# Attention scores of nine head pairs in three float32r passes, splits on GpSimd, sums' transfers on SyncE, a new order within a head pair

## The chip, the cores and the metric

The kernel runs on one core of one Trainium2 chip. The metric is the device time of one execution in microseconds, the median of the runs. Tiles have up to 128 partitions; TensorE multiplies a stationary tile (its weights) with moving columns and writes PSUM, which has eight banks of 512 float32 a partition; VectorE and ScalarE read PSUM, GpSimd works on SBUF alone, and SyncE issues transfers.

## What is computed

Attention with an additive bias of relative position, followed by a gated feed-forward block. Batch 4, 8 heads, 576 positions, head width 64, model width 512, inner width 1024, all float32.

```python
scores = scale * np.matmul(q, k.transpose(0, 1, 3, 2))
...
x = (psi_rel / psi_i)[..., None]
h = np.maximum(x @ w1 + b1, 0.0)
bias = h @ w2
scores = scores + bias.transpose(2, 0, 1)[None, :, :, :]
scores = scores - np.max(scores, axis=-1, keepdims=True)
attn = np.exp(scores)
attn = attn / (np.sum(attn, axis=-1, keepdims=True) + 1e-09)
return np.matmul(attn, v).astype(np.float32)
...
h = np.maximum(x @ w_in, 0.0)
...
    conv_out += conv_w[k][None, None, :] * hp[:, k:k + S, :]
gate = 1.0 / (1.0 + np.exp(-conv_out))
return (h * gate @ w_out).astype(np.float32)
```

## The kernel before

Three stages follow each other. In the first (to about 62 us) the bias of all heads is computed and written to DRAM; in the second (to about 282 us) attention runs; in the third the feed-forward block. The weights of the third are prepared beside the second.

Attention runs over 16 head pairs, `seq[n]` = (pair of heads p, batch b), b the faster index. The 576 queries of a pair are cut into five units: t = 0 holds the first 64 queries of both heads in one tile, t = 1 to 4 hold 128 queries each, once for each head h. One unit and head passes through these steps:

- `S` (`scores`, lines 421 to 445): queries as weights, keys as moving columns. The 576 keys lie as two halves of 288, the first on partitions 0 to 63 (a = 0), the second on 64 to 127 (a = 1), so that two matmuls of 64 rows lie side by side in the array and write the two banks of one pair of PSUM banks. The operands are float32. The unit t = 0 uses 64 columns of weights for each head, so that four matmuls lie side by side.
- `R` (`reduce`, line 452, VectorE): adds the bias tile, scales, and finds the row's extreme value, from PSUM into SBUF.
- `E` (`expo`, line 466, ScalarE): the exponential, with its row sum.
- `T` and `s` (`transposes`, `side_transposes`): 64-column transposes of the unit on TensorE as float32r, into another pair of banks; `k0`, `k1`, `k0b`, `k1b` and `c` copy them to SBUF (line 149 ScalarE, line 152 VectorE).
- `P` (`pv_parts`): the product with the values, for query columns 0 to 319 (g = 0, tile `ptx`) and 320 to 575 (g = 1, tile `pty`), five parts each; `xb` copies it out.
- `ia`, `inv`, `sm`, `rt`, `st`, `sp`, `AN`: the sums of a pair are inverted, turned, copied, stored to DRAM (`store_sums`), read back spread over partitions (`spread_sums`), and multiplied in by GpSimd (`apply_norm`, line 617).

The order of all this within one pair is written out by hand in the string `CYCLE` (line 863): each entry names a step, its unit, head and pair offset, and the engine that it runs on (P TensorE, V VectorE, A ScalarE, G GpSimd). Every engine takes its instructions in that order. The pairs of PSUM banks are given out by `take` and `done` (lines 406 to 417): a step takes, of the free pairs, the one touched longest ago, where free is judged in program order; on the chip the step then waits for those that used the pair last. `side_cols` puts side columns into spare columns of the pair of the last scores.

Queries and keys are loaded on SyncE's queue (`load`, line 205) two pairs ahead, after the step `S:4,1`; values after `P:1,4`. The bias rows of the next p are loaded as soon as the last batch's reduction of a unit has freed the tile (`load_bias`, line 231): t = 0 on SyncE's queue, t = 1 to 4 on GpSimd's, except for the first p. The sums' transfers are issued by GpSimd.

The 28 weight jobs (`job_step`, `J1`, `J2`, `J3`, `W`; `per_pair` says how many lie in each pair) bring weights into a pair of float32r tiles: VectorE shifts (line 158), ScalarE and VectorE put the parts together (159, 163), and GpSimd rounds into the first tile and subtracts for the second (lines 191, 192). The feed-forward block multiplies float32 numbers as three float32r products of such tiles (high x high, high x low, low x high; `in_products`, `ffn_out`). `x_parts` splits the attention output on GpSimd the same way.

At the end of attention, `apply_norm` of the last pairs, `split_x` of the last two weight tiles and `x_rest` (lines 637 to 645) follow on GpSimd, and TensorE multiplies the remaining 64 columns of each batch (tile `xr`) from them.

Of the kernel before, what the change touches and what calls it, by code (L numbers as in the profile page):

```python
# [9 lines left out]
F32 = mybir.dt.float32  # L10
# [8 lines left out]
def attention_ffn_kernel(  # L19
# [43 lines left out]
    arena = nc.alloc_sbuf_tensor("shared", [P, SPB * SPW], F32)  # L63
# [4 lines left out]

    sps = [[shared_at(f"s{x}{i}", [P, SPW], dt, i * SPW) for i in range(SPB)] for x, dt in (("p", F32), ("r", F32R))]
# [125 lines left out]
    with tc.manual_schedule():  # L195
        att = ExitStack()
        q_p = pool(att, "q", 2)
# [7 lines left out]
        def load(n):  # L205
            p, b = seq[n]
            qks[n] = t = q_p.tile([P, KO + S], F32, name="qk")
            keys = qk[b, p, :, KO:].rearrange("d (h a s) -> d a h s", h=2, a=2)
            for a in range(2):
                rows = slice(D * a, D * a + D)  # L210
                nc.sync.dma_start(t[rows, 0:KO], qk[b, p, :, 0:KO])
                nc.sync.dma_start(halves(t[rows, KO:]), keys[:, a])

# [14 lines left out]
        def load_bias(p, t, cuts=()):  # L231
            queue = nc.gpsimd if p and t else nc.sync
# [188 lines left out]
        def scores(n, t, h):  # L421
# [179 lines left out]
        def store_sums(n):  # L601
            rt = rts.pop(n)
            rows = r_d[n, :, TL:].rearrange("h (t x) -> h t x", x=P)
            nc.gpsimd.dma_start(rows, rt[0:8])  # L604
            nc.gpsimd.dma_start(r_d[n:n + 1, :, 0:TL], rt[8:9].rearrange("o (h x) -> o h x", h=2))

        def spread_sums(n):
            rbs[n] = rb = rb_p.tile([P, S], F32, name="rb")
            for h in range(2):
                nc.gpsimd.dma_start(rb[D * h:D * h + D], r_d[n, h:h + 1, :].to_broadcast([D, S]))  # L610
# [171 lines left out]
        slots += [[0, i - 4, 0] for i in range(4)]  # L782
        hs_ff = {}
# [45 lines left out]
        per_pair = [0, 0, 3, 0, 3, 3, 3, 0, 3, 3, 3, 0, 3, 3, 1, 0]  # L829
# [20 lines left out]
        def job_step(j, k):  # L850
# [6 lines left out]
            if k == 2:  # L857
                if j in first_job and first_job[j] % B == 0:
# [5 lines left out]
            E:1,0,0:A S:2,0,0:P S:2,1,0:P S:3,0,0:P E:1,1,0:A R:2,0,0:V S:3,1,0:P T:0,0:P R:2,1,0:V J1:0,0:V  # L864
            k1:0,0:V J2:0,0:A P:1,0,-1:P R:3,0,0:V P:1,1,-1:P E:2,0,0:A k0:0,0:A P:1,2,-1:P E:2,1,0:A R:3,1,0:V
# [384 lines left out]
```

## Time and profile before

| | |
|---|---|
| median of 3 runs | 478.18 us (477.30 to 478.56) |
| the profiled execution | 478.16 us |
| its span, first to last instruction | 476.3 us |
| TensorE matmul busy | 460.4 us (97%) |
| VectorE, ScalarE, GpSimd busy | 350.1, 312.1, 143.6 us |
| granted TensorE clock | 1.00 throughout |
| TensorE's share of the chain that ended last | 86% |

The page shows one execution. Each engine's busy time is the union of its instructions' spans; an instruction's span holds its latency, so back-to-back instructions start closer together than their mean duration. The chain that ended last is followed back from the last instruction, at each step to what released it or to the instruction before it on its engine; the time of a piece in it is what it adds to the chain, and "x8" counts instruction records. A float32 matmul appears as two records, a float32r matmul as one.

### The profile page before, as it was taken

The page shows a single profiled execution, that of the slowest core. Times are in us where ns is not written, and L with a number is a line of the kernel's source. Part 1 is how long each engine was busy: PE and PEld are TensorE (multiplying, and loading weights), DVE is VectorE, ACT ScalarE, POOL GpSimd, SP SyncE. Part 2 cuts the span into 40 slices and gives each one's busy share as a digit, 9 for nine tenths or more (in the row PEclk, how much of TensorE's full clock was granted, in tenths as well). Part 3 has the DMA queues.
Part 4 walks back from the last instruction along what each step waited for, and adds up shares of the span by engine and source line. Part 5 has one row for each costly group of instructions (what it writes and reads, how often), then busy time and mean ns, then how long its engine had stood idle before and what let it go on. Part 6 is the DMA issues. An engine that isn't in the chain of part 4 may idle for free.

```text
span 476.3 us, 10546 instructions
## 1 busy us (share of the span) xinstructions
PE 460.4 (97%) x3915; PEld 334.1 (70%) x3915; DVE 350.1 (73%) x847; ACT 312.1 (66%) x740; POOL 143.6 (30%) x216
## 2 busy tenths in 40 slices
PE   5988899999999999999999999999999999999996
PEld 3333356677667766777667778988888888888886
DVE  6999967887898799987897521892599149936971
ACT  6999876888888788988888632861354126414530
POOL 1000001344656544464568528006001500060000
PEclk9999999999999999999999999999999999999999
DMA  1799957796978968798951300002000200020002
GB/s 38 224 339 317 344 169 179 194 283 142 242 176 198 294 145 211 170 268 195 222 130 51 115 27 26 0 1 82 7 1 0 89 23 0 1 89 1 0 14 98
DMA packets 32774, 60.79 MB, mean 128 GB/s; under 512 B 7196, under 2 KB 15796, under 8 KB 32724
## 3 DMA queue, kind: packets, MB, share of 16 engines
q1 hardware_dynamic: 27860, 47.90, 36.2%
q0 software_dynamic: 4480, 11.88, 8.9%
q8 instruction: 31, 0.51, 0.5%
q10 hardware_dynamic: 384, 0.35, 0.3%
q14 instruction: 19, 0.16, 0.1%
HBM read 44.12 MB, written 15.98 MB: 126 GB/s over the span
## 4 chain that ended last, share of the span: by engine, by line
PE 86%; DVE 4%; ACT 3%; DMA 3%; POOL 2%; issue 1%; SPq 0%; POOLq 0%; DVEq 0%
PE bank L105 38%; PE pair L105 36%; PE bank L108 10%; DVE y L308 2%; DMA bias_d<-st 2%; PE pair L108 2%; DVE sp L452 1%; ACT st L351 1%; ACT y L304 1%; DMA pars<-in_par_dram 1%; ACT tl L351 1%; DMA bt<-bias_d 1%; POOL x L617 1%; ACT sp L466 0%; POOL xr L645 0%
## 5 line engine op out<-in xcount | busy, mean ns | idle before, releaser
L452 DVE CUSTOM_DVE_ANT_0 sp<-pair,bt 128x576 f32<-128x576 f32 x144 | 104.5, 750 | 27.0 <-PE pair L105 24.5
L466 ACT ACTIVATE sp<-sp,nm 128x576 f32<-128x576 f32 x144 | 110.4, 771 | 11.9 <-DVE nm L452 11.5
L105 PE MATMUL pair<-qk 64*128 64x288 f32 (+1 forms) x640 | 88.8, 426 | 2.1 <-DVE nm L452 2.0
L105 PE MATMUL pair<-xs,wi 128*128 128x512 f32 x384 | 88.9, 390 | 0.0
L105 PE MATMUL bank<-wo,g 128*128 128x512 f32 x384 | 87.7, 389 | 0.0
L105 PEld LDWEIGHTS bank<-wo,g 128*128 128x128 f32 x384 | 72.0, 188 | 14.9
L105 PEld LDWEIGHTS pair<-xs,wi 128*128 128x128 f32 x384 | 71.7, 188 | 15.3 <-issue 0.4
L108 PE MATMUL bank<-identr,sr 64*128 64x64 f32 x1184 | 65.9, 253 | 2.2 <-ACT sp L466 2.0
L108 PEld LDWEIGHTS bank<-identr,sr 64*128 64x128 f32 x1184 | 56.3, 136 | 14.1 <-issue 4.6
L1043 DVE SCALAR_TENSOR_TENSOR cv<-h,cw,cv 128x575 f32<-128x575 f32 x64 | 52.3, 818 | 12.6 <-ACT cv L1038 10.6
L105 PEld LDWEIGHTS pair<-qk 64*128 64x128 f32 (+1 forms) x640 | 47.3, 175 | 17.6 <-DVE nm L452 6.8
L666 ACT ACTIVATE h<-pair 128x512 f32<-128x512 f32 x32 | 19.1, 598 | 58.0 <-PE pair L105 58.0
L308 DVE TENSOR_SCALAR y<-tl,inv,nb 128x576 f32<-128x576 f32 (+33 forms) x112 | 47.5, 498 | 0.0
L105 PE MATMUL bank<-ptx,vt 128*64 128x320 f32 x320 | 47.0, 438 | 0.0
L105 PE MATMUL pair<-y,pars 128*32 128x512 f32 (+8 forms) x352 | 42.5, 504 | 1.7 <-DVE y L308 1.0
L191 POOL TENSOR_SCALAR xs<-x 128x512 fp32r<-128x512 f32 (+1 forms) x16 | 11.2, 700 | 103.7 <-DVE gt L1063 103.6
L105 PE MATMUL bank<-pty,vt 128*64 128x256 f32 x320 | 38.1, 384 | 0.0
L604 POOL DMA_DIRECT2D r_d<-rt x16 | 9.7, 606 | 90.1 <-DVE rt L152 90.1
L105 PEld LDWEIGHTS bank<-ptx,vt 128*64 128x64 f32 x320 | 21.4, 136 | 22.0 <-ACT ptx L149 3.1
L1049 ACT ACTIVATE cv<-cv 128x576 f32<-128x576 f32 x32 | 21.9, 684 | 21.9 <-DVE cv L1043 21.8
L1050 DVE SCALAR_TENSOR_TENSOR cv<-cv,h 128x576 f32<-128x576 f32 x32 | 24.1, 752 | 14.1 <-ACT cv L1049 14.1
L105 PEld LDWEIGHTS pair<-y,pars 128*32 128x32 f32 x352 | 15.8, 114 | 25.7 <-DVE y L308 10.2
(84 smaller groups left out, 600.1 us busy)
## 6 DMA issues: line engine op xcount, KB each, us to landing
qk<-in_qk_dram SPq DMA_DIRECT2D x32, 320.0 KB, 5.0
bias_d<-st SPq DMA_DIRECT2D x13, 607.0 KB, 5.9
bt<-bias_d POOLq DMA_DIRECT2D x24, 288.0 KB, 6.0
qk<-in_qk_dram SPq DMA_DIRECT2D x32, 144.0 KB, 5.1
rb<-r_d POOLq DMA_DIRECT2D x32, 144.0 KB, 5.1
vt<-in_v_dram SPq DMA_DIRECT2D x16, 256.0 KB, 4.0
raw_w<-in_moe_w_in_dram SPq DMA_DIRECT2D x16, 256.0 KB, 5.0
out_dram<-o SPq DMA_DIRECT2D x16, 256.0 KB, 2.0
```

Of the source, the lines that this page charges most:

```text
L105: return use(nc.tensor.matmul(o, *args, **kw), o)
L108: return use(nc.tensor.transpose(o, *args), o)
L191: first = nc.gpsimd.tensor_scalar(dst[:, 0], x, 1.0, 0.0, op0=ALU.mult, op1=ALU.add)
L308: nc.vector.tensor_scalar(y, dist[:, 0:n], inv[:, ig:ig + 1], nb1, op0=ALU.mult, op1=ALU.max)
L351: use(nc.scalar.activation(o[:, :, oo], i[:, :, ii], AF.Identity, bias=kv[:, k:k + 1], scale=inv_scale), ps)
L452: use(nc.vector.tensor_tensor_reduce(out=halves(spt[n, t][0][:, h]), in0=ps[:, :, 0:HS], in1=halves(bt[:, h]), op0=ALU.add, op1=ALU.min, s ...
L466: exps[n, t, h] = nc.scalar.activation(sp[:, h], sp[:, h], AF.Exp, bias=nm[:, h:h + 1], scale=-1.0, accum_out=sms[n][:, col:col + 1],)
L604: nc.gpsimd.dma_start(rows, rt[0:8])
L666: use(nc.scalar.activation(h[:, 0:NM], ps[:, 0], AF.Relu), ps)
L1043: nc.vector.scalar_tensor_tensor(out=cv[:, o:o + S - 1], in0=h[:, i:i + S - 1], scalar=cw[:, f, kk:kk + 1], in1=cv[:, o:o + S - 1], op0=AL ...
L1049: nc.scalar.activation(cv, cv, AF.Tanh, scale=0.5)
L1050: nc.vector.scalar_tensor_tensor(out=cv, in0=cv, scalar=1.0, in1=h, op0=ALU.add, op1=ALU.mult)
```

## The change

For nine head pairs (n = 3, 4, 6, 7, 8, 10, 11, 12, 14) queries and keys are split by GpSimd into a rounded part and a remainder, and the scores are three float32r passes (high x high, high x low, low x high) in place of a float32 matmul. In these pairs the unit t = 0 multiplies two zero-padded sets of 128 weight columns into the same bank, one after the other. The two high tiles take the place of the raw tiles of `raw_p`; queries and keys and their low parts lie in the shared arena, as do, later, the last two `wo` tiles, the output tiles and `hr`. The split's steps `X` are in the `CYCLE` of the pair before. The sums are stored and spread on SyncE's queue, and the bias rows of t = 1 and 2 of a later p are loaded there. `CYCLE` has a new order of its steps, some copies go to another engine, and the weight jobs are spread otherwise over the pairs.

```diff
...
+    QKW = 2 * (P + NT * P) + S
+    QAT = SPB * SPW
+    arena = nc.alloc_sbuf_tensor("shared", [P, QAT + 2 * QKW], F32)
...
+    qk_t = [[shared_at(f"q{x}{i}", [P, QKW], dt, QAT + i * QKW) for i in range(2)] for x, dt in (("k", F32), ("l", F32R))]
...
-            qks[n] = t = q_p.tile([P, KO + S], F32, name="qk")
+            qks[n] = t = qk_t[0][n % 2]
             keys = qk[b, p, :, KO:].rearrange("d (h a s) -> d a h s", h=2, a=2)
             for a in range(2):
                 rows = slice(D * a, D * a + D)
-                nc.sync.dma_start(t[rows, 0:KO], qk[b, p, :, 0:KO])
-                nc.sync.dma_start(halves(t[rows, KO:]), keys[:, a])
+                for ins in (
+                    nc.sync.dma_start(t[rows, 0:KO], qk[b, p, :, 0:KO]),
+                    nc.sync.dma_start(halves(t[rows, KO:]), keys[:, a]),
+                ):
+                    if n - 2 in scored:
+                        tc.add_manual_dep(ins.ins, scored[n - 2].ins.name, DATA)
...
+        his, scored = [], {}
+        chunks = [slice(KO, KO + S), slice(0, QW), slice(QW, KO)]
+
+        def is_split(n):
+            return n > 2 and n % B != 1 and n + 1 < NSEQ
+
+        def split_qk(n, k):
+            x, lo, hi, cs = qks[n], qk_t[1][n % 2], his[(n + 1) % 2], chunks[k]
+            nc.gpsimd.tensor_scalar(hi[:, cs], x[:, cs], 1.0, 0.0, op0=ALU.mult, op1=ALU.add)
+            nc.gpsimd.tensor_sub(lo[:, cs], x[:, cs], hi[:, cs].bitcast(F32))
...
-            queue = nc.gpsimd if p and t else nc.sync
+            queue = nc.gpsimd if p and t not in (0, 1, 2) else nc.sync
...
-            for hh, qo, po in ops:
-                for a in range(2):
-                    rows = slice(D * a, D * a + D)
-                    mm(
-                        ps[po, a, 0:HS],
-                        qt[rows, qo:qo + po.stop - po.start],
-                        qt[rows, KO + hh * HS:KO + hh * HS + HS],
-                        start=True,
-                        stop=True,
-                    )
+            parts, one = [(qt, qt)], bool(t) or not is_split(n)
+            if is_split(n):
+                hi, lo = his[(n + 1) % 2], qk_t[1][n % 2]
+                if not t:
+                    ops = [(hh, hh * QW, slice(0, P)) for hh in range(2)]
+                parts = [(hi, hi), (hi, lo), (lo, hi)]
+            for i, (left, right) in enumerate(parts):
+                for hh, qo, po in ops:
+                    for a in range(2):
+                        rows = slice(D * a, D * a + D)
+                        scored[n] = mm(
+                            ps[po, a, 0:HS],
+                            left[rows, qo:qo + po.stop - po.start],
+                            right[rows, KO + hh * HS:KO + hh * HS + HS],
+                            start=(i == 0 and (one or hh == 0)),
+                            stop=(i == len(parts) - 1 and (one or hh == 1)),
+                        )
...
-            nc.gpsimd.dma_start(rows, rt[0:8])
-            nc.gpsimd.dma_start(r_d[n:n + 1, :, 0:TL], rt[8:9].rearrange("o (h x) -> o h x", h=2))
+            nc.sync.dma_start(rows, rt[0:8])
+            nc.sync.dma_start(r_d[n:n + 1, :, 0:TL], rt[8:9].rearrange("o (h x) -> o h x", h=2))
...
-                nc.gpsimd.dma_start(rb[D * h:D * h + D], r_d[n, h:h + 1, :].to_broadcast([D, S]))
+                nc.sync.dma_start(rb[D * h:D * h + D], r_d[n, h:h + 1, :].to_broadcast([D, S]))
...
+        his += [raw_p.tile([P, QKW], F32R, name=f"hi{i}", tag="raw") for i in range(2)]
...
-        per_pair = [0, 0, 3, 0, 3, 3, 3, 0, 3, 3, 3, 0, 3, 3, 1, 0]
+        per_pair = [0, 0, 2, 2, 3, 2, 2, 1, 3, 2, 2, 1, 3, 2, 2, 1]
...
         CYCLE = """
-            E:1,0,0:A S:2,0,0:P S:2,1,0:P S:3,0,0:P E:1,1,0:A R:2,0,0:V S:3,1,0:P T:0,0:P R:2,1,0:V J1:0,0:V
-            k1:0,0:V J2:0,0:A P:1,0,-1:P R:3,0,0:V P:1,1,-1:P E:2,0,0:A k0:0,0:A P:1,2,-1:P E:2,1,0:A R:3,1,0:V
-            P:1,3,-1:P k0b:0,0:V J3:0,0:V P:1,4,-1:P T:1,0:P k1b:0,0:V xb:1,-1:V ia:-1:A inv:-1:V s:1,0:P
-            E:3,1,0:A T:2,0:P E:3,0,0:A k1:1,0:A c:1,0:V S:4,0,0:P S:4,1,0:P k0:1,0:V sm:-1:P k0:2,0:A J1:2,0:V
-            s:2,0:P s:3,0:P R:4,0,0:V T:3,0:P c:2,0:V J2:2,0:A rt:-1:V k1:2,0:A R:4,1,0:V S:0,0,1:P J3:2,0:V
-            P:0,0,0:P P:0,1,0:P R:0,0,1:V E:4,1,0:A inv:-3:V W:0,0:G E:4,0,0:A k0:3,0:A P:0,2,0:P c:3,0:V
-            P:0,3,0:P P:0,4,0:P k1:3,0:V s:4,0:P S:1,0,1:P W:2,0:G xb:0,0:A AN:-3:G S:1,1,1:P J1:4,0:V T:4,0:P
-            sp:-2:G J2:4,0:A st:-1:G R:1,0,1:V E:0,0,1:A J3:4,0:V c:4,0:A k0:4,0:A R:1,1,1:V k1:4,0:A W:4,0:G
+            E:1,1,0:A X:0,1:G E:1,0,0:A S:2,0,0:P R:2,0,0:V S:2,1,0:P S:3,0,0:P X:1,1:G S:3,1,0:P ia:-1:A
+            X:2,1:G R:2,1,0:V E:2,0,0:A s:1,0:P T:0,0:P k0:0,0:A P:1,0,-1:P R:3,1,0:V P:1,1,-1:P k1:0,0:A
+            E:2,1,0:A P:1,2,-1:P R:3,0,0:V P:1,3,-1:P inv:-2:V E:3,1,0:A P:1,4,-1:P k1b:0,0:A k0b:0,0:V T:1,0:P
+            AN:-3:G xb:1,-1:V inv:-1:V S:4,0,0:P S:4,1,0:P E:3,0,0:A J1:0,0:V k1:1,0:A s:2,0:P c:1,0:V k0:1,0:A
+            T:2,0:P R:4,0,0:V R:4,1,0:V T:3,0:P J2:0,0:A S:0,0,1:P c:2,0:V k1:2,0:V E:4,0,0:A S:1,0,1:P k0:2,0:A
+            J1:2,0:V E:4,1,0:A R:0,0,1:V S:1,1,1:P k1:3,0:A k0:3,0:V sm:-1:P J3:0,0:V s:4,0:P W:0,0:G J2:2,0:A
+            sp:-2:G s:3,0:P T:4,0:P J3:2,0:V P:0,0,0:P P:0,1,0:P rt:-1:A R:1,1,1:V k1:4,0:V W:2,0:G J1:4,0:V
+            J2:4,0:A J3:4,0:V W:4,0:G k0:4,0:A P:0,2,0:P R:1,0,1:V E:0,0,1:A P:0,3,0:P st:-1:G c:4,0:A P:0,4,0:P
+            c:3,0:A xb:0,0:V
         """.split()
...
+            elif k == "X":
+                if is_split(n):
+                    split_qk(n, t)
...
+        def split_wo(k):
+            tc.add_manual_dep(split_x(wo[FE + k], ws[k]).ins, scored[NSEQ - 1].ins.name, DATA)
...
```

## Rows read from the trace of the kernel before

**Rows 1.** The page: busy time of each engine, and one of its groups.

```profile
PE 460.4 (97%) x3915; PEld 334.1 (70%) x3915; DVE 350.1 (73%) x847; ACT 312.1 (66%) x740; POOL 143.6 (30%) x216
...
L105 PE MATMUL pair<-qk 64*128 64x288 f32 (+1 forms) x640 | 88.8, 426 | 2.1 <-DVE nm L452 2.0
```

**Rows 2.** Chain that ended last, attention: start us, us added, what, records.

```profile
132.34 0.65 PE pair L105 x8
...
136.01 1.07 PE pair L105 x7
...
137.68 2.05 PE pair L105 x15
...
140.06 2.31 PE bank L105 x20
...
143.23 0.68 PE bank L108 x16
...
145.83 0.65 PE pair L105 x8
...
254.07 0.65 PE pair L105 x8
```

**Rows 3.** The chain in two short stretches of the FFN: 256 columns, then 512.

```profile
299.98 4.08 PE pair L105 x34
...
335.84 4.31 PE pair L105 x19
```

**Rows 4.** Busy us (instructions) of PE, PEld, DVE, ACT, POOL in one period; clock, DMA.

```profile
132.34:145.83 13.49, 13.49 (x168) 9.46 (x171) 12.45 (x36) 11.98 (x32) 7.03 (x11) 1.00 0.72 175
```

**Rows 5.** Timeline, two stretches: start us, us, engine, line, operation.

```profile
188.43 1.41 POOL L617 TENSOR_TENSOR x<-x,rb 128x576 f32<-128x576 f32 x1
...
188.57 1.42 DVE L158 TENSOR_SCALAR wu<-raw_w 128x256 int32<-128x256 int32 x1
...
197.69 1.25 PE L105 MATMUL pair<-qk 64*128 64x288 f32 x8
...
198.03 0.29 DVE L158 TENSOR_SCALAR wu<-raw_w 128x256 int32<-128x256 int32 x1
198.49 0.76 DVE L452 CUSTOM_DVE_ANT_0 sp<-pair,bt 128x576 f32<-128x576 f32 x1 [0.17 <-PE pair L105]
```

**Rows 6.** Groups by line and shape: count, busy us, mean ns of one, idle before.

```profile
L158 DVE TENSOR_SCALAR wu<-raw_w 128x256 int32<-128x256 int32 x28 | 16.4, 587 | 0.0
...
L192 POOL TENSOR_TENSOR wo<-wu,wo 128x256 fp32r<-128x256 f32 x12 | 8.8, 732 | 1.0
...
L192 POOL TENSOR_TENSOR xs<-x,xs 128x576 fp32r<-128x576 f32 x4 | 5.7, 1428 | 0.3
...
L191 POOL TENSOR_SCALAR wo<-wu 128x256 fp32r<-128x256 f32 x12 | 4.9, 408 | 22.7 <-DVE wu L163 22.6
...
L191 POOL TENSOR_SCALAR xs<-x 128x576 fp32r<-128x576 f32 x4 | 2.7, 669 | 0.1
```

**Rows 7.** SyncE's issues by time, and the landing of all loads of queries and keys.

```profile
172.00 0.47 SPq L211 DMA_DIRECT2D qk<-in_qk_dram  x1
...
173.82 0.62 SPq L212 DMA_DIRECT2D qk<-in_qk_dram  x1
...
176.82 4.63 SPq L178 DMA_DIRECT2D raw_w<-in_moe_w_out_dram  x3
...
198.97 0.47 SPq L211 DMA_DIRECT2D qk<-in_qk_dram  x1
...
DMA to landing us min/median/max: 3.9/5.1/11.7
```

**Rows 8.** Timeline at the end of attention; idle us before and releaser in brackets.

```profile
283.30 0.60 POOL L604 DMA_DIRECT2D r_d<-rt  x1 [8.69 <-DVE rt L152]
...
293.63 0.19 PEld L105 LDWEIGHTS pair<-xr,wi 128*128 128x128 f32 x1 [0.25 <-POOL xr L644]
...
294.44 2.78 PE L105 MATMUL pair<-xr,wi 128*128 128x256 f32 x21 [0.42 <-POOL xr L645]
```

More of the change, by code (lines that the diff above doesn't have):

```diff
@@ L62, in attention_ffn_kernel @@
     SPW = 2 * S + 8
-    arena = nc.alloc_sbuf_tensor("shared", [P, SPB * SPW], F32)
+    QKW = 2 * (P + NT * P) + S
+    QAT = SPB * SPW
+    arena = nc.alloc_sbuf_tensor("shared", [P, QAT + 2 * QKW], F32)
     base = nc.lookup_mloc(arena).addr
@@ L196, in attention_ffn_kernel @@
         att = ExitStack()
-        q_p = pool(att, "q", 2)
         qk_p = pool(att, "qk", 2)
@@ L857, in job_step @@
             if k == 2:
-                if j in first_job and first_job[j] % B == 0:
+                if j in first_job and first_job[j] % B == 0 and ("S", 4, 1, first_job[j]) not in begun:
                     held.append((load_job, j + 3))
@@ L945, in emit @@
                 if (g, c) == (1, 4) and n + 2 < NSEQ:
-                    if seq[n][1] == B - 1:
+                    if seq[n][1] == B - 1 and ("S", 4, 1, n + 1) not in begun:
                         held.append((load_v, n + 2))
@@ L1023, in attention_ffn_kernel @@
         ff = ExitStack()
-        wo_p = pool(ff, "wo", 1)
         g_p[0] = pool(ff, "g", FC + 4)
         e2_p = pool(ff, "e2", 2)
-        hr_p = pool(ff, "hr", 1)
-        o_p = pool(ff, "oo", 3)
-        wo += [wo_p.tile([P, 2, DM], F32R, name=f"wo{f}") for f in range(FE, FC)]
+        HAT = 2 * P * FC + FC * (B - 1) * TL
+        wo += [shared_at(f"wo{f}", [P, 2, DM], F32R, HAT + 2 * DM * (f - FE)) for f in range(FE, FC)]
+        outs = [shared_at(f"o{i}", [P, DM], F32, HAT + 2 * DM * (FC - FE) + DM * i) for i in range(3)]
         gt = [shared_at(f"gt{f}", [P, 2, P], F32R, f * 2 * P) for f in range(FC)]
@@ L1071, in ffn_out @@
                     )
+        stored = []
         def store(ps, dst, eng):
-            o = o_p.tile([P, ps.shape[1]], F32, name="o")
+            o = outs[len(stored) % 3][:, 0:ps.shape[1]]
+            stored.append(o)
             if eng:
@@ L1105, in run @@
                         stage(b * FC + j - k, k)
-        hr += [shared_at(f"hr{f}", [P, B - 1, TL], F32, 2 * P * FC + f * (B - 1) * TL) for f in range(FC - 1)]
-        hr.append(hr_p.tile([P, B - 1, TL], F32, name="hr"))
+        hr += [shared_at(f"hr{f}", [P, B - 1, TL], F32, 2 * P * FC + f * (B - 1) * TL) for f in range(FC)]
         ws = [narrow(tp, raw_o[0][:, k], ("cv", "cv")) for k, tp in enumerate((e_p, e2_p))]
@@ L1111, in attention_ffn_kernel @@
         x_rest(0)
-        split_x(wo[FE], ws[0])
+        def split_wo(k):
+            tc.add_manual_dep(split_x(wo[FE + k], ws[k]).ins, scored[NSEQ - 1].ins.name, DATA)
+        split_wo(0)
         for b in range(1, B):
@@ L1116, in attention_ffn_kernel @@
             x_rest(b)
-        split_x(wo[FE + 1], ws[1])
+        split_wo(1)
         for b in range(B):
@@ L1121, in attention_ffn_kernel @@
                 main_out(ahead[2], 0, 2)
+                if wide() is not ahead[2]:
+                    wide()
                 for f in range(3, 6):
```

## The prediction

> **What bounds the kernel.** I read the busy table first, then the chain of work that ended last, then that chain within one pair of heads. TensorE is busy for 97% of the span [rows 1], but that figure proves little, because the ends of matmuls are modelled. The chain decides: inside one head pair it is TensorE from end to end [rows 2]. From one t=0 score to the next (132.34 to 145.83 us) it takes 13.49 us, and from there to pair 15 (254.07) nine such periods take 13.5 us each. In the same stretch VectorE is busy 12.45 us, ScalarE 11.98 and GpSimd 7.03 [rows 4]. So a microsecond taken off TensorE is worth a microsecond until VectorE, about one microsecond behind, becomes the bound. The profiled execution took 478.16 us (span 476.3, the rest lies around it), as good as the median 478.18; sums are made against 478.16.
>
> **Price of a score before.** Two heads are 8 records and 1.07 us, four are 2.05 us [rows 2]. The difference gives 0.485 us per head, so one pair of records (the two 64-row halves side by side) takes 0.2425 us, and every group of scores pays about 0.10 us on entry. Each float32 matmul is two records (640 [rows 1] for 320 calls in the code). The t=0 unit has 8 records, four side by side, 0.65 us, of which 0.165 is entry.
>
> **Price of a pass after.** A float32r matmul is one record. In the FFN, 512 columns take 4.31/19 = 0.2268 us and 256 columns 4.08/34 = 0.120 us [rows 3]. A line through both (0.417 ns a column, the 2.4 GHz level, which the granted clock of 1.00 [rows 4] is, plus 13 ns) gives 0.1334 us for 288 columns. For two halves side by side with their own weights no such row exists. Lower bound: the columns alone, 0.120. Upper bound: the transposes, also float32r on two halves, take 0.68 us for 8 slots [rows 2], 0.085 a slot for 64 columns, 0.045 above the line; added to 0.1334 that is 0.178. I take 0.1334, since the FFN rows stream a like number of columns and the transposes stream only 64.
>
> **Slots.** Per split pair: eight heads of t>0, each 3 passes instead of 0.485, 8 x (0.400 - 0.485) = -0.68. At t=0 the four-way form is lost: 2 heads x 3 passes = 6 slots = 0.80 instead of 0.485, +0.32. Net -0.36 us, over nine pairs **-3.3 us**.
>
> **Group entries.** The new order has three groups of scores a pair instead of four (t=0 and t=1 stand together). A float32 group costs 0.10 to 0.165 to enter. Float32r scores behind float32r transposes may enter for nothing or pay the same 0.10. Saved per split pair 0.15 to 0.45; I take 0.3, **-2.7 us** over nine. The other five pairs in steady order save one entry, **-0.5 us**.
>
> **The splits.** Three chunks (576, 640, 640 columns), each a rounding copy and a subtraction on GpSimd. At 576 these take 0.669 and 1.428 us [rows 6]; at 640 I estimate 0.74 and 1.57 from the 256- and 576-column rows. Together 6.7 us per split pair. GpSimd loses four transfer issues of some 0.6 us [rows 8] and one weight job (1.1 us), so it goes from 7.0 to about 10.4 of 12.8 us. That fits, if it is early enough. Keys and queries are loaded after the last score of the pair two ahead: the fourth transfer starts 1.8 us after the first and lands some 5.1 us later [rows 7]. Counting from the first score of unit 2, TensorE's order is 12 slots (1.6), unit 0's transposes (0.5 with a side column), PV of the pair before (2.3), unit 1's transposes (0.8) and six slots (0.8): the last score ends at 6.0. The load starts 0.2 to 0.3 us later [rows 5, 7], at 6.3, and lands at 13.2, 0.4 us into the next cycle of 12.8. The splits then end at 7.1 to 7.3, with the seams between them; the t=0 score starts at 7.5 and reads the last chunk's low part at 8.1. Cost nothing, 0.8 us of cover; if it is gone, every microsecond of lateness is one of TensorE.
>
> **GpSimd against VectorE.** This is the cost I cannot read off one row. The weight job's first step (a shift, line 158) took 0.29 us alone and 1.42 us when a GpSimd operation on SBUF had begun 0.14 us before it [rows 5]; the mean of 28 is 0.587 [rows 6], so about a quarter were long. The Trainium skill, "SBUF — State Buffer", section "SBUF: two separate sides", states it as a rule: the port pair that VectorE and GpSimd share is locked for a whole instruction, and the later one waits. That trace agrees (1.42 us, ending 0.15 us after the GpSimd operation). Now GpSimd works through the first 7.3 us of a cycle, then the normalising multiply until about 8.7, and the two shifts lie at 5.1 and 8.1.
> Who waits for them? I followed the bank pairs by the allocator's rule. Unit 2's transposes take the pair that the copy of unit 1's side column frees, right behind the first shift. They are due at 6.1. PV ends at 4.5, its evacuation (0.4) at 5.0, then the shift: with a short one the copy (0.29) is done at 5.6, with a full long one at 6.8, 0 or 0.7 us lost. Unit 4's transposes take the pair that the t=0 reduction frees; they are due at 9.4 (6.1 plus two transposes 1.35, twelve slots 1.6, side columns 0.3). The reduction starts 0.22 us after its scores [rows 5], at 8.5, and ends at 9.3; behind a long second shift it ends 0.3 to 0.5 us late. Lower bound 0 (a wait here gives nothing back), upper bound 1.2 us a cycle, 10.8 in all. How long a shift waits depends on where in an operation it falls. By the times above the first falls at the end of a copy, just before a subtraction, and each 0.1 us lost in a cycle brings the next load, and with it the splits, 0.1 us earlier against that cycle. So I take 0.2 us: **+1.8 us**.
>
> **The rest.** ScalarE gives one 512-column copy to VectorE and takes small ones: 11.98 us less a job step; VectorE's 12.45 loses two job steps (0.7) and gains that copy (0.6): both fit in 12.8, VectorE barely where shifts are long. The weight jobs stay 28, only spread otherwise. Sums' transfers on SyncE's queue: four issues of 0.5 to 0.6 us a pair, in a queue that issued three loads in 4.63 us after a burst [rows 7]; the spread waits for the multiply of the pair before, behind it stand only a weight load for a later job and the store. Bias rows of units 1 and 2 go the same way, three times. Cost nothing. In the tail GpSimd stood behind the store of the last sums (8.69 us idle) with two multiplies and the rest columns behind it, and TensorE waited twice, 0.25 and 0.42 us [rows 8]. With the store elsewhere the first multiply moves up and the chain ends before TensorE comes: **-0.6 us**. The buffers that move into the shared arena wait for the last scores, long past by then: nothing.
>
> **Sum.** -3.3 - 2.7 - 0.5 + 1.8 - 0.6 = -5.3: **472.9 us**.
>
> **Rivals.**
> 1. *The shared port takes it back* (ends slower). Both shifts long in all nine cycles: -7.1 + 10.8 = +3.7, 481.9. It decides from 0.8 us of stall a cycle. For it: GpSimd is busy at both places. Against: four of the nine cycles still hold float32 units 2 to 4 and are 0.3 us longer, with that much cover, and two have one job only. Half of it gives 476.5. Chance 0.18.
> 2. *The weights of a pass don't hide*: 0.178 a slot, 30 slots = 5.3 against 4.37, +0.97 a pair. +8.8 - 2.7 - 0.5 - 0.6 = +5.0: 483. Break-even near 0.16. For it the 0.085 us slots of the transposes; against, 256 columns at 0.120 us on the same rows of the array. The Trainium skill, "TensorE: Matmul & The Clock Gate", section "Part 3: Packing small matmuls — row/col tiling", has it that a weight load overlaps running matmuls only in other row groups; by it the slots would lie near the upper bound, and the 0.120 us rows, whose loads and matmuls all take the same 128 rows, speak against it. Chance 0.09. That the change doesn't do what it says, with the two halves one after the other, would be 0.267 a slot, +33 us; the four records side by side in 0.65 us [rows 2] speak against it: 0.02.
> 3. *The splits come late*: load landing was 11.7 us at worst [rows 7]. 0.5 us late in each of nine cycles leaves 477.4. Chance 0.08.
> 4. *It does all it can*: no stall and 0.122 a slot, -7.1 - 3.0: 468. Chance 0.08.
>
> **How the numbers follow.** The forecast, 470 to 476, has 0.55. A difference under 0.3% (1.4 us) can hardly be told from none. Faster than 476.7: forecast and rival 4 (0.63), 0.03 of rival 1 and 0.05 of rival 3, 0.71; within 0.3%: 0.09 of rival 1 and 0.03 of rival 3, 0.12; slower: 0.06 of rival 1 and rival 2 (0.11), 0.17. The range 469 to 480 leaves out rival 4's end, rival 2 and the worst of rival 1.
>
> **What would show it.** One period between t=0 scores near 12.8 to 13.0 us for pairs 6, 7, 10 and 11 (13.49 before); score slots at 0.133 us (0.178: rival 2); TensorE idle before the transposes of units 2 and 4 below 0.3 us a cycle, else rival 1, with line 158's mean above 0.8; idle before t=0 scores: rival 3. I am wrong if the slot is right and the period isn't.

## The result and the profile after

The changed kernel takes 480.6 us (480.15 to 480.81, 4 runs) against 477.74 (4 runs): 1.0058, interval 1.0038 to 1.0079, 0.6% slower. The forecast was 472.9, "faster" with 0.71. The profiled execution took 480.15 us (span 478.3), 2.0 more than the one of before (478.16); the account below is made with these two.

The page after, and TensorE's score slots (timeline: start, us of one group, records), to be held against [rows 1, 2]:

```profile
PE 458.1 (96%) x4095; PEld 342.1 (72%) x4095; DVE 350.9 (73%) x818; ACT 314.4 (66%) x769; POOL 162.9 (34%) x194
...
PE 74%; DMA 11%; DVE 8%; issue 3%; ACT 2%; POOL 1%; SPq 0%; DVEq 0%
...
106.42 0.30 PE L108 MATMUL pair<-hi 64*128 64x288 f32 x2
106.55 0.30 PE L108 MATMUL pair<-ql,hi 64*128 64x288 f32 x2
106.68 0.30 PE L108 MATMUL pair<-hi,ql 64*128 64x288 f32 x2
```

TensorE has less to do (458.1 against 460.4 us), and a pass starts 0.132 us after the one before it, where 0.1334 was forecast (the mean inside the groups; the second slot of a group starts 0.23 to 0.24 after the first, which is 0.10 of what a group pays to enter). But TensorE's share of the chain fell from 86 to 74%, and DMA (11 against 3%) and VectorE (8 against 4%) take its place. The chain of before:

```profile
PE 86%; DVE 4%; ACT 3%; DMA 3%; POOL 2%; issue 1%; SPq 0%; POOLq 0%; DVEq 0%
```

The period that was to be 12.8 to 13.0 us is this one, from pair 9's product to pair 10's (the chain; start, us added, what):

```profile
199.45 0.90 PE pair L108 x12
...
200.38 1.35 PE bank L111 x32
201.73 1.69 PE pair L108 x24
...
204.45 2.84 PE bank L108 x20
207.30 1.79 PE pair L108 x24
```

The chain is TensorE's from end to end, and the period takes 13.1 us. A slot costs what was forecast, so 12 slots are 1.58 us, and the three groups pay 0.11, 0.11 and 0.21 to enter: 0.42, against 0.47 for the four of [rows 2]. Of the 0.3 a cycle, 0.05 was saved.

Not every period is so clean. The table gives, for each pair, the us from the pair before's first product into `pty` to its own (the same point of every cycle, idx 2 to 14; "clean" is about the shortest that its kind reaches in the runs below, to within 0.03; the columns to its right are the runs of experiments 1, 2, 3, 9 (first), 4 (first) and 7 (first)).

| pair | before | after | clean | later shift | bias SyncE | both | even jobs | float32 | before, sums SyncE |
|---|---|---|---|---|---|---|---|---|---|
| 2 | 13.48 | 13.98 | 13.28 | 13.60 | 13.51 | 13.74 | 13.56 | 14.31 | 20.70 |
| 3 | 13.50 | 14.17 | 13.09 | 13.11 | 13.60 | 13.09 | 13.10 | 14.65 | 13.49 |
| 4 | 13.49 | 13.62 | 13.42 | 13.82 | 13.62 | 13.83 | 13.41 | 14.14 | 13.49 |
| 5 | 13.48 | 13.66 | 13.28 | 13.26 | 13.65 | 13.29 | 13.28 | 13.61 | 13.49 |
| 6 | 13.50 | 13.96 | 13.09 | 13.62 | 13.84 | 13.29 | 13.34 | 13.60 | 13.50 |
| 7 | 13.48 | 13.09 | 13.09 | 13.08 | 13.09 | 13.08 | 13.09 | 13.60 | 13.48 |
| 8 | 13.48 | 13.87 | 13.42 | 14.41 | 13.63 | 13.83 | 13.43 | 13.80 | 13.48 |
| 9 | 13.50 | 13.68 | 13.28 | 13.28 | 13.67 | 13.29 | 13.29 | 13.61 | 13.50 |
| 10 | 13.49 | 13.14 | 13.09 | 13.11 | 13.52 | 13.10 | 13.12 | 13.60 | 13.48 |
| 11 | 13.48 | 13.25 | 13.09 | 13.34 | 13.11 | 13.53 | 13.64 | 13.61 | 13.49 |
| 12 | 13.82 | 15.03 | 13.42 | 14.77 | 14.09 | 13.82 | 13.44 | 13.80 | 13.50 |
| 13 | 13.49 | 13.67 | 13.28 | 13.29 | 13.64 | 13.28 | 13.29 | 13.60 | 13.49 |
| 14 | 13.48 | 13.52 | 13.42 | 13.44 | 13.67 | 14.02 | 13.43 | 14.15 | 13.48 |
| sum | 175.7 | 178.6 | 172.3 | 176.1 | 176.6 | 175.2 | 173.4 | 180.1 | 182.6 |

(Pairs 3, 6, 7, 10 and 11 have passes throughout the period; 2, 5, 9 and 13 float32 scores in unit 4 only; 4, 8, 12 and 14 in units 0 to 3 of the pair that follows.) Clean cycles would have won 3.1 us on before's 13 times 13.49; waits of 6.4 us took that back twice over. Two of them as the trace shows them, the first in the timeline at 106 us (in brackets idle before it and what ended it), the second in the chain into period 12:

```profile
106.12 1.75 DVE L161 TENSOR_SCALAR wu<-raw_w 128x256 int32<-128x256 int32 x1
106.27 1.44 POOL L641 TENSOR_TENSOR x<-x,rb 128x576 f32<-128x576 f32 x1
107.80 0.74 DVE L476 CUSTOM_DVE_ANT_0 sp<-pair,bt 128x576 f32<-128x576 f32 x1
108.60 0.42 PE L111 MATMUL bank<-identr,sr 64*128 64x64 f32 x6 [1.04 <-DVE nm L476]
```

```profile
215.41 0.58 POOL bt L256
...
216.55 1.42 POOL x L641
217.97 0.51 POOL bt L256
218.48 10.03 DMA bt<-bias_d
```

In the first, the second shift (0.29 us alone) met the multiply and took 1.75 us; the t=0 reduction behind it in VectorE's queue came late, and unit 4's transposes, which take its banks, waited 1.04. (From here on a wait of TensorE is told from the start of one matmul to the start of the next, 1.29 in this place; the idle time in the brackets is shorter.) The same wait stands at 135.9, 149.8, 190.5 and 245.6 us, 3.4 us in the five starts together beyond their usual spacing. In the second, GpSimd issued the last of unit 4's bias rows only behind the splits, the rows of unit 3 and the multiply; it took 10 us to land, and unit 4's reduction waited for it.

### The profile page after: what moved, and what is told of

Same layout as the page of the kernel before. It is cut to its first block, busy times and chain, and to the rows that moved or that the text cites. A ratio compares the mean times of both kernels' runs of the same rounds, so it can differ in the third digit from the quotient of the medians.

```text
span 478.3 us, 10920 instructions
## 1 busy us (share of the span) xinstructions
PE 458.1 (96%) x4095; PEld 342.1 (72%) x4095; DVE 350.9 (73%) x818; ACT 314.4 (66%) x769; POOL 162.9 (34%) x194
## 4 chain that ended last, share of the span: by engine, by line
PE 74%; DMA 11%; DVE 8%; issue 3%; ACT 2%; POOL 1%; SPq 0%; DVEq 0%
PE bank L108 35%; PE pair L108 31%; PE bank L111 7%; DMA bt<-bias_d 4%; DMA bias_d<-st 3%; DVE sp L476 2%; DVE y L325 2%; DVE ptx L155 1%; DMA vt<-in_v_dram 1%; ACT y L321 1%; DMA raw_w<-in_moe_w_in_dram 1%; ACT st L368 1%; DMA qk<-in_qk_dram 1%; DMA pars<-in_par_dram 1%; DVE pty L155 1%
## 5 line engine op out<-in xcount | busy, mean ns | idle before, releaser
L111 PE MATMUL bank<-identr,sr 64*128 64x64 f32 x1184 | 60.5, 245 | 5.1 <-DVE nm L476 3.0
L111 PEld LDWEIGHTS bank<-identr,sr 64*128 64x128 f32 x1184 | 53.8, 136 | 14.6 <-issue 5.8
L231 POOL TENSOR_SCALAR hi<-qk 128x640 fp32r<-128x640 f32 (+1 forms) x27 | 19.2, 711 | 83.6 <-DMA qk<-in_qk_dram 79.4
L108 PE MATMUL pair<-qk 64*128 64x288 f32 (+1 forms) x280 | 40.6, 433 | 4.0 <-DVE nm L476 2.7
L232 POOL TENSOR_TENSOR ql<-qk,hi 128x640 fp32r<-128x640 f32 (+1 forms) x27 | 41.0, 1517 | 2.3
L152 ACT ACTIVATE ptx<-bank 128x256 f32<-128x256 f32 (+2 forms) x92 | 39.1, 460 | 1.5 <-PE bank L111 0.8
```

The source lines that it names most:

```text
L108: return use(nc.tensor.matmul(o, *args, **kw), o)
L111: return use(nc.tensor.transpose(o, *args), o)
L152: return noted(nc.scalar.activation(o, i, AF.Copy), i)
L231: nc.gpsimd.tensor_scalar(hi[:, cs], x[:, cs], 1.0, 0.0, op0=ALU.mult, op1=ALU.add)
L232: nc.gpsimd.tensor_sub(lo[:, cs], x[:, cs], hi[:, cs].bitcast(F32))
```

## The experiments

**1. The later second shift.** In `CYCLE`, `J1:2` goes from ahead of the t=0 reduction to behind it and two copies; nothing else changes.

```diff
-            J1:2,0:V E:4,1,0:A R:0,0,1:V S:1,1,1:P k1:3,0:A k0:3,0:V sm:-1:P
+            E:4,1,0:A R:0,0,1:V S:1,1,1:P k1:3,0:A k0:3,0:V J1:2,0:V sm:-1:P
```

> The second weight job's shift moves behind the t=0 reduction and a copy on VectorE; nothing else changes. Theory A: in the changed kernel this shift waits for GpSimd's normalising multiply (1.1 to 1.7 us in six cycles), the t=0 reduction stands behind it, and the transposes of unit 4 wait for that reduction, 3.4 us in five cycles (0.93 to 1.29 us gaps where 0.1 is usual). So the five waits go and the time falls from 480.6 to 477.2, give or take 0.8. Rival B: VectorE has no time left in a cycle anyway and the wait only moves to the next copy that TensorE needs: 480 to 481.

477.71 us, 1.0013 [0.9985, 1.0041]; 2.9 less than after, as theory A had it. The waits at unit 4's transposes are gone. At the same place of its trace:

```profile
105.33 1.44 POOL L641 TENSOR_TENSOR x<-x,rb 128x576 f32<-128x576 f32 x1
105.64 0.76 DVE L476 CUSTOM_DVE_ANT_0 sp<-pair,bt 128x576 f32<-128x576 f32 x1 [0.51 <-ACT ptx L152]
106.93 0.28 DVE L161 TENSOR_SCALAR wu<-raw_w 128x256 int32<-128x256 int32 x1
```

The reduction, which reads PSUM, takes 0.76 us beside the multiply as it does alone; the shift, which works on SBUF, now comes behind it and takes 0.28. The Trainium skill, "SBUF — State Buffer", section "SBUF: two separate sides", has VectorE (in instructions of certain kinds) and GpSimd lock their common port for a whole instruction, the first to start getting it. The length agrees (1.75 us, to 0.16 behind the multiply's end); the order doesn't, as recorded, for the shift that was held started 0.15 us ahead of the multiply, and no run here settles why.

The other cause isn't touched by this edit and shows more: in period 8, now 14.41, the last bias row takes 10.34 us to land and stands in the chain; period 12 stays at 14.77.

**2. All bias rows on SyncE's queue.**

```diff
-            queue = nc.gpsimd if p and t not in (0, 1, 2) else nc.sync
+            queue = nc.sync
```

> Bias rows of units 3 and 4 also go to SyncE's queue. Theory A: in the changed kernel the last of them was issued by GpSimd behind the splits and the multiply and landed 10 us later, and a reduction waited 1.5 us; issued at once it lands in time: 479.2. Rival: the transfer engines are full there and it lands late all the same: 480.6. The waits before unit 4's transposes stay in both.

477.66 us, 0.9991 [0.9978, 1.0004]; 2.9 less than after, more than expected. Period 12 falls to 14.09, and periods 2 and 3 by half a microsecond each; those were not foreseen. The waits of unit 4's transposes are still there, 0.6 to 1.0 us each, but in period 3 it is 0.74 where it was 1.29. Period 2's half isn't the edit's doing: it is TensorE's wait for the first weight load, 0.93 us in the kernel after and 0.46 here (0.52 and 0.69 in experiments 1 and 3). These runs issue that load at the same point, 7.34 us behind pair 0's product, before anything that the edits move, and it lands sooner or later.

**3. Both edits.**

> The kernel after with both single edits: the second weight shift (J1:2) behind VectorE's copy, and all bias rows on SyncE. Each alone took 2.9 us off the kernel after (480.6 to 477.7). Theory A, the port wait and the late bias row are two costs at different places (unit 4's transposes; the late bias row at cycle 12 and the crowded start at cycles 2 and 3): the gains add, 474.8, between 474.0 and 475.8, the interval of cycle 12 near 13.8 and of cycle 3 near 13.1. Theory B, the two edits remove the same stalls by moving GpSimd's work earlier or VectorE's later: not below 477.

477.59 us, 1.0009 [0.9989, 1.0029]: theory B by the median, which did not move. The periods' sum says half of each: 176.1 and 176.6 alone, 175.2 together, where independent gains would have given 174.1. Of the missing 1.1 us 0.6 is period 2's weight load, which no edit touches, and 0.5 lies in period 3, where both edits shorten the same wait; the other periods' differences cancel. What is left stands in the table: 2, 11 and 14 half a microsecond above clean, and 4, 8 and 12 at 13.83. In period 4 the chain is VectorE for five microseconds before TensorE's wait:

```profile
120.98 0.75 DVE sp L476
...
121.74 0.60 DVE pty L155
122.34 0.32 DVE wu L161
...
122.76 0.84 DVE wu L166
123.61 0.67 DVE sp L476
...
124.34 1.73 PE pair L108 x12
```

Periods 4, 8 and 12 are the cycles with three weight jobs.

**4. The new order without any passes,** once with all else as after, once in the kernel before (its `CYCLE` replaced, without the `X` steps).

```diff
-            return n > 2 and n % B != 1 and n + 1 < NSEQ
+            return False
```

> The changed kernel with no head pair split: all scores are float32, the order, the queues, the spread of the jobs and the buffers stay. Theory A: the new order saves no entry into a group of scores (a period with float32 scores in it took 13.5 to 13.6 us without waits), the tail gains 0.8 us, the start loses 0.8, and without splits the multiply runs early and meets no shift: 477.5 to 478.5, so that the three passes with their splits cost the 2 to 3 us by themselves. Rival C: the order and the queues cost the time, and the three passes gain as foreseen: 482 or more.

> The kernel before with the new order of a head pair alone: no split, sums and bias rows on GpSimd as before, weight jobs as before. My prediction's entry term says one group entry less a cycle, 0.3 us: period 13.2 and 474 to 475. Theory B, from the run with float32 scores (clean period 13.60): the merged group pays as much for entering as the two did, the order costs 0.1 us a cycle, 479 to 480, and more if VectorE's shifts meet GpSimd, 481 to 483.

482.2 us, 1.0086 [1.0066, 1.0107], and 514.39, 1.0759 [1.0738, 1.078]. The first total is rival C's: order and queues without passes are slower than with them. Its periods hold 3.3 us over thirteen clean ones of 13.60, mostly in 2, 3, 4 and 14, without a single split of queries and keys: in period 3 a shift of 1.86 us is followed by a wait of 1.27, and in period 2 TensorE waits 0.93 for the first weight load. So the splits are not the only source of the waits. In both, the undisturbed periods take 13.58 to 13.61 us, 0.11 more than before's 13.49. The groups of scores in the second:

```profile
167.80 1.07 PE pair L105 x8
...
170.23 1.82 PE pair L105 x16
...
175.73 2.14 PE pair L105 x16
```

Two heads behind transposes pay 0.10 as before (1.07). The merged group of t=0 and t=1 takes 1.82 where the two of [rows 2] took 0.65 + 1.07 = 1.72: merging saves no entry, it adds 0.10. Units 2 and 3, now directly behind the product with the values, take 2.14 instead of 2.05. Transposes win 0.07 back. So the entry term was wrong in sign with float32 scores, and the passes only bring it back to about zero. That it is the neighbour that sets the price is read from these rows; no run changes the neighbour alone.

The 514 us hold something else: three waits of 8.3 to 8.6 us, in pairs 5, 9 and 13. The chain before the first:

```profile
131.07 0.44 SPq L211
...
132.88 0.62 SPq L212
...
133.54 4.78 DMA raw_w<-in_moe_w_in_dram
...
138.42 0.09 DVE wu L158
```

Behind the new position of the first shift, VectorE waits for a weight load that `held` puts behind four loads of keys and queries. The kernel after, with its own spread of jobs and the condition on `begun`, has no such wait. So this run's total says nothing of the order; its undisturbed periods do.

**5. Splits of pairs 3 and 4 only.** The later pairs multiply what lies in the two tiles, and all three passes are high x high; so most of GpSimd's split work and the passes' low parts are left out, with as many matmuls.

```diff
-                parts = [(hi, hi), (hi, lo), (lo, hi)]
+                parts = [(hi, hi), (hi, hi), (hi, hi)]
...
-                if is_split(n):
+                if n in (3, 4):
```

> GpSimd splits only the first two of the nine head pairs; the others multiply what those left, high by high in each of the three passes, so the scores are not the reference's. TensorE's work is the same, GpSimd is rid of some 47 us. Theory A: the waits of TensorE before the transposes of unit 4 (3.4 us) and the late bias rows (1.2 us) come from GpSimd's work, and go: 475.5 to 476.5. Rival B or C: the waits come from VectorE's load or from the queues and stay: 479.5 to 481.

478.87 us, 1.0021 [1.0003, 1.0039], between the two. Periods 5, 6, 7, 10, 11 and 13 are clean (13.25, 13.13, 13.11, 13.13, 13.10, 13.28): in 5, 6, 11 and 13, which were up to 0.8 longer, it was GpSimd's split work that made the waits. Periods 2 and 3, where the splits remain, are as bad as after (14.10, 14.09), and 8 and 12 stay at 13.8, the VectorE cycles of experiment 3. Periods 9 (13.71) and 14 (14.08) aren't clean either: in 14 a shift of 1.31 us met GpSimd's split of the attention output, and unit 4's transposes waited 0.74.

**6. The old order with passes,** the splits at the start of its cycle; then with the bias rows on SyncE.

> The kernel after with the old order of a head pair; the three chunks of the split stand at the start of GpSimd's cycle, all else is as in the kernel after. Theory A, the new order saves no group entry and costs 0.1 us a cycle by itself (13.60 against 13.49 with float32 scores) plus waits of unit 4's transposes: with the old order a full split period is at most 13.0 to 13.1 and the time is 475 to 477, below the kernel after by 3.5 to 5.5 us, the late bias row at cycle 12 still there. Theory B, my prediction's entry term (the new order saves 0.3 us a cycle): at least 2.7 us slower than the kernel after's clean cycles, 13.4 a cycle, 481 or more. Theory C, the old order leaves the splits no room before the t=0 scores, or meets the shift and copies with GpSimd elsewhere: waits ahead of the first score of the pair, 479 or more with split cycles above 13.4.

> The old order with split pairs, and all bias rows on SyncE. If the late bias rows cost this order what they cost the new one (2.9 us), 2.9 below the run with the old order alone, some 473; if GpSimd's queue in the old order takes bias rows in time, no difference beyond 0.5 us. Between the two: only cycle 12's wait goes, 1.2 us.

486.79 us, 1.0191 [1.0161, 1.0221], and 490.38 (484.17 to 493.86, the profiled execution being the longest), 1.0226 [1.0156, 1.0297]. Period 2 takes 17.90 and 21.05 us, for the reason of experiment 7, so the totals say nothing of the order. In periods 4, 8 and 12 of the first run the old order reaches 13.3, 0.1 below the new one; those with passes throughout take 13.70, 14.10, 13.64, 16.33 and 13.39, with TensorE waiting 0.5 to 0.9 us for copies and reductions that stand behind shifts, 0.65 to 1.5 us long, in the splits. The 16.33 is not waiting alone: the granted clock was 0.57 from 207 to 211 us. So by these runs the new order costs 0.1 us a cycle; that in exchange it keeps more of VectorE's work out of the splits' way is argued from the first run's waits, and no run separates it.

**7. The sums' transfers.** Three runs: before with all of them on SyncE; before with only the last pair's; and experiment 3's kernel with those of pairs 0 to 2 back on GpSimd.

```diff
+        def sums_q(n):
+            return nc.sync if n == NSEQ - 1 else nc.gpsimd
...
-            nc.gpsimd.dma_start(rows, rt[0:8])
+            sums_q(n).dma_start(rows, rt[0:8])
```

> The kernel before with the sums' transfers alone moved to SyncE's queue. My prediction's step: nothing in the steady cycles, 0.6 to 0.8 us off the tail: 477.0 to 477.3. Rival, SyncE blocks behind the spread at the start (in the kernel after the spread of the first pair waits for the store's landing and holds up the first weight load and the key loads): cycles 2 and 3 longer by 0.5 us each and the time 477.7 to 479.

> The kernel before with only the last pair's sums' transfers on SyncE. In the run with all of them there, the first spread held up the first weight load, VectorE waited for it, TensorE stood 2.65 us and its granted clock fell to the 1.2 GHz level until about 102 us: 7.2 us lost in cycle 2. If that is the whole loss, this run keeps the 13.48 us of cycle 2 and gains the tail's 0.6 to 0.8 us: 477.0 to 477.2. If the tail's gain in the kernel after came from something else (the arenas), no difference: 477.8.

> The run with the later shift and the bias rows on SyncE, with the sums of pairs 0 to 2 back on GpSimd's queue. Theory A, SyncE's blocking at the start still costs it something: cycle 1 to 2 falls by 0.2 to 0.7 us (the 0.69 us wait of unit 1's transposes at 90.3 goes), 477.0. Theory B, nothing left there: 477.6.

482.5 us, 1.0104 [1.0063, 1.0145]: one edit that was costed at nothing takes 4.6 us by itself. The chain of that run, then busy us of PE, PEld, DVE, ACT and POOL, granted clock and DMA in its stretches:

```profile
82.54 1.63 DMA r_d<-rt
...
84.75 0.58 SPq L610
...
85.39 3.55 DMA raw_w<-in_moe_w_in_dram
...
88.97 0.29 DVE wu L158
89.59 0.67 DVE sp L452
...
91.72 1.20 PE bank L108 x12
```

```profile
90.00:93.00 3.00, 2.42 (x36) 2.30 (x38) 2.94 (x12) 3.00 (x11) 1.14 (x2) 0.70 0.64 191
93.00:96.00 3.00, 3.00 (x29) 2.81 (x28) 1.61 (x6) 1.66 (x4) 0.00 (x0) 0.50 0.01 1
102.00:106.50 4.50, 4.50 (x58) 3.44 (x54) 3.14 (x9) 4.01 (x10) 1.27 (x3) 1.00 0.35 98
```

The spread waits on SyncE for the store to land, the first weight load stands behind it, the first shift waits for that load, and copies and reductions stand behind the shift in VectorE's queue. TensorE waited 2.65 us; then its granted clock was 0.50, the 1.2 GHz level, until a little before 102 us. Period 2 took 20.70 us, 7.2 more, and of that only some 3 us are waiting. The kernel after has the same chain (the weight load issued at 85.84, the shift at 90.52) but its order puts less behind the shift; its wait there is 0.93 us and its clock stays.

With only the last pair's transfers moved (the edit shown): 476.98 us, 0.9986 [0.9977, 0.9996]. The start keeps its 13.48; from pair 15 to the end the profiled span is 198.6 us against 199.2: the tail's gain, alone. The third run, 479.83, 1.0044 [1.0026, 1.0063], went against both theories. GpSimd:

```profile
85.97 1.07 POOL L637 DMA_DIRECT2D rb<-r_d  x2 [3.47 <-DMA r_d<-rt]
87.06 0.70 POOL L231 TENSOR_SCALAR hi<-qk 128x576 fp32r<-128x576 f32 x1
...
92.61 1.55 POOL L232 TENSOR_TENSOR ql<-qk,hi 128x640 fp32r<-128x640 f32 x1
```

It stood 3.47 us for the store's landing, with the six split operations behind it (they start at 80.8 with the sums on SyncE). TensorE waited 1.4 and 1.0 us for them, its clock fell again (0.53 from 95 to 98 us), and period 2 took 16.93. Either queue blocks; what differs is who stands behind.

**8. All pairs from 3 to 14 split,** on top of experiment 3.

> The run with the later shift and the bias rows on SyncE, and now also pairs 5, 9 and 13 split, so that pairs 3 to 14 all use three passes. In that run a full split cycle took 13.09 us, a cycle with float32 scores in units 0 to 3 took 13.83 (VectorE is the chain for 5 us there and TensorE waits 0.53 us for a reduction), one with float32 unit 4 13.28. Theory A, TensorE is the bound and GpSimd has room: the intervals 4, 5, 8, 9, 12, 13 all fall to 13.1, 2.8 us off, 474.8 by the median. Theory B, GpSimd or the loads have no room in those cycles (the first of a new weight of bias and values): the splits come late or the multiply meets the shifts, intervals stay above 13.4 and the time is not below 477.

484.68 us, 1.0125 [1.0064, 1.0186]: theory B, as far as pairs 5, 9 and 13 go. In the profiled execution (479.90, the shortest of the four) periods 5, 9 and 13 fall to 13.2, but 4, 8 and 12 rise to 14.8, 15.2 and 16.2. In period 12 the load of queries and keys, issued at 214.35 to 216.9, lands 6 us behind its last issue, and the splits are late with it:

```profile
216.26 0.62 SPq L215 DMA_DIRECT2D qk<-in_qk_dram  x1
...
222.77 0.67 POOL L231 TENSOR_SCALAR hi<-qk 128x576 fp32r<-128x576 f32 x1 [4.64 <-DMA qk<-in_qk_dram]
...
228.28 0.40 PE L108 MATMUL pair<-hi 64*128 64x288 f32 x2 [0.88 <-POOL hi L231]
229.91 0.40 PE L108 MATMUL pair<-hi,ql 64*128 64x288 f32 x2 [0.75 <-POOL ql L232]
```

TensorE waits 1.3 and 1.0 us for a high and a low part, and 1.0 in period 8. That is the prediction's rival 3, in the pairs that the change leaves out. In period 4 no score waits for a split: its two waits of 0.7 us are for a copy and a reduction of VectorE's.

**9. Even jobs; then both shifts later.** On top of experiment 3, and the second on top of the first.

```diff
-        per_pair = [0, 0, 2, 2, 3, 2, 2, 1, 3, 2, 2, 1, 3, 2, 2, 1]
+        per_pair = [0, 0, 2, 2, 2, 2, 2, 2, 2, 2, 2, 2, 2, 2, 2, 2]
...
-            AN:-3:G xb:1,-1:V inv:-1:V S:4,0,0:P S:4,1,0:P E:3,0,0:A J1:0,0:V k1:1,0:A s:2,0:P c:1,0:V k0:1,0:A
+            AN:-3:G xb:1,-1:V inv:-1:V S:4,0,0:P S:4,1,0:P E:3,0,0:A k1:1,0:A s:2,0:P c:1,0:V J1:0,0:V k0:1,0:A
```

> The run with the later second shift and the bias rows on SyncE, and now the 28 weight jobs as two in each of pairs 2 to 15, instead of three in pairs 4, 8 and 12 and one in 7, 11 and 15. Theory A, VectorE becomes the bound for some 5 us in the cycles with three jobs (intervals 13.83, 13.82, 13.82, one wait of 0.53 us each for a reduction): these three fall to 13.4, the ones that get a second job stay at 13.1, 1.0 to 1.3 us off: 476.4. Theory B, the wait comes from the float32 scores themselves and not from the third job: no change in them, 477.6 or more, since pairs 7, 11 and 15 get a job more.

> As the run with even jobs, and the first shift (J1:0) moved behind the copy of unit 1's side column (c:1), which frees the banks that unit 2's transposes wait for. Theory A, all that keeps the kernel after from its own clean cycles are stalls: clean intervals are 13.28 (2, 5, 9, 13), 13.09 (3, 6, 7, 10, 11) and 13.41 (4, 8, 12, 14), 6.5 us less than the kernel after has in these thirteen, 480.6 - 6.5 = 474.1, and no wait of TensorE above 0.4 us is left between 95 and 275 us. Theory B, a shift that starts later meets the splits' or the multiply's other operations, or holds up the reductions of unit 4 behind it: intervals stay where they were, 476.5 or more.

476.83 us, 0.9976 [0.9953, 0.9999], and 476.0, 0.9977 [0.9953, 1.0002], beside before at 477.5. The first did what theory A says: periods 4, 8 and 12 fall to 13.41 to 13.44, 1.2 us together, pair 7 carries a second job for nothing, and the periods' sum is 173.4, 1.2 above clean. Another 0.6 us come from period 14, whose pair had two jobs already; why isn't shown. The second removes the waits for the side column's copy (period 2 at 13.26, 11 from 13.64 to 13.49), but period 6 rises to 13.89: TensorE starts when GpSimd's last low part is done.

```profile
145.77 1.57 POOL ql L232
...
147.38 1.20 PE pair L108 x14
```

The sum stays at 173.6, so one wait was traded for another; 474.1 is not reached. Part of the distance is not attention's: the profiled execution of the second run enters attention 1.5 us later than that of before, behind a stage that the edits don't touch; in it the granted clock was 0.66 from 50 to 55 us, where before has 1.00 throughout.

## Why the prediction was wrong

| term | forecast | measured | from |
|---|---|---|---|
| slots | -3.3 | -3.6 | 9 x (30 x 0.132 - 9 x 0.485) |
| entries | -3.2 | +0.5 | clean periods, 172.3 - 175.4 = -3.1, less the slots |
| stalls | +1.8 | +6.4 | periods 178.6 - 172.3 |
| tail | -0.6 | -1.2 | from pair 14 to the end |
| rest | 0 | 0.0 | +0.3 before pair 1's product; -0.3, a late row of before in its own period 12 |
| sum | -5.3 | +2.1 | 2.0 in the profiled executions |

*Bound.* Right: undisturbed periods are TensorE's alone, before and after. "A microsecond until VectorE becomes the bound" was right too, but I compared averages; VectorE became the bound first in the three cycles with three jobs, where I had given it room.

*Slots.* Right: 0.132 us, both halves side by side, weights hidden. Rival 2 falls. With it falls the Trainium skill's rule as I applied it ("TensorE: Matmul & The Clock Gate", "Part 3: Packing small matmuls — row/col tiling"): by it I put the slots near 0.178, an estimate. In the trace the weights of the next slot load while the matmuls of the same rows run, and a slot takes 0.132.

*Group entries.* This step failed: wrong by 3.7 of the 7.4 us between the forecast and the measured difference, and in its sign. It came from no row: I counted groups, took 0.10 to 0.165 as the price of one wherever it stands, and let two groups become one. Experiment 4's rows have 0.10 behind transposes and 0.20 behind the product with the values, and four-way and two-way scores in one group still pay, 0.10 more than in two. [Rows 2] had the warning: 0.165 for t=0 and 0.10 for t=1 were different prices. The lower bound of 0.15 saved should have been a cost.

*Stalls.* This step was wrong by 4.6 us, more than the entries. One mechanism was right, its price not: rival 1's place (the second shift in the multiply, the reduction behind it, unit 4's transposes) is in the trace five times, at 0.6 to 1.3 us. I took 0.2 us a cycle from a wait-free schedule in which the splits end at 7.3 and the multiply at 8.7; experiment 1 is worth 2.5 us of periods, 0.4 of it period 2's weight load. My mark for rival 1, the shift's mean above 0.8, failed: the mean is 0.591 against 0.587. In the kernel before, shifts were as long, at places where nobody waited. The total came out near rival 1's 481.9, but the port is only part of it: of the 6.4 us, the shift and the bias rows make 3.4 together (experiment 3, 0.2 of it the weight load), the even spread of the jobs takes 1.8 (experiment 9: 1.2 in the cycles with three jobs, 0.6 in period 14), and 1.2 were not taken away. The bias rows and the spread of the jobs were put at nothing.

*Bias rows* "cost nothing" was wrong, and for the rows that did not move: units 3 and 4 stayed on GpSimd's queue, now behind 6.7 us of splits. I had priced the rows that the change moves, not those behind what it adds.

*Sums* "behind it stand only a weight load for a later job": wrong. That load's job was VectorE's next instruction (in experiment 7's first run VectorE stood idle 3.42 us for it), and VectorE's queue holds TensorE's banks. In the kernel after TensorE's wait for it is 0.93 us; in the old order the cycle lost 7.2 (experiment 7).

*Splits*: right. In the kernel after no score waits for a split; experiments 8 and 9 show how thin the 0.8 us of cover are. *Tail*: right, but twice the size. TensorE meets the rest columns without the two waits of [rows 8], and half a microsecond of the 1.2 comes from the last pair's transfers alone (experiment 7); no run separates the rest.

That experiments 1 and 2 together give 3.4 and not 4.5 us of periods lies in periods 2 and 3 (experiment 3); beyond that, in both the multiply and the shifts move in time, and which shift meets which GpSimd operation changes. The three parts of the 6.4 hold only for this order of the edits.

## What to carry to other kernels

Price a group by the row that has the same neighbour before it, not by a mean over places; an entry that "disappears" needs a row that shows it. Of every queue to which work is added, list what stays on it behind the new work, and follow each waiting instruction one queue further, to what its engine has behind it. Compare engines' loads cycle by cycle: the cycle with one job more is where the next bound appears.

## What was not expected of the hardware

A wait of 2.65 us of TensorE cost 7.2 us: its granted clock went from 1.00 to 0.50 and came back some ten microseconds later (experiment 7); after a wait of 8.3 us it was 0.57 over the next seven (experiment 4):

```profile
131.00:139.00 8.00, 0.06 (x4) 0.03 (x2) 0.58 (x3) 0.76 (x2) 0.00 (x0) 0.73 0.66 155
139.00:146.00 7.00, 7.00 (x74) 5.24 (x76) 5.11 (x15) 3.50 (x9) 1.59 (x3) 0.57 0.20 75
```

The waits of the kernel after, up to 1.3 us, left it at 1.00, and so did two of 1.3 and 1.0 us close together in experiment 8; the two of 1.4 and 1.0 us in experiment 7's third run did not (0.53 over three us), nor did waits of at most 0.9 us in experiment 6's first (0.57 over four). So the size of a wait alone doesn't tell whether the clock falls.

It falls in single executions too, and this blurs the medians. In experiment 1 the five executions with a mean granted clock of 0.998 or more took 476.8 to 477.5 us, the five below it 477.9 to 482.9. Of experiment 9's first run the four at 0.998 or more took 474.3, 474.7, 475.3 and 476.5, beside a median of 477.4 for the 18 of before; chosen after the fact, these are a hint of a gain near 2 us where the medians have 0.7.

A bias row issued by GpSimd took 10.03 us to land. In before unit 4's rows took up to 9.2 and, in period 12, 11.1 us as well; they had only been issued earlier.
